# Block-sparse attention feeding a top-1 mixture of experts, one core: pairs of an expert's token slots share one splitting of its weights

## The chip, the core and the metric

The kernel runs on one core of one Trainium2 chip. The metric is device time of one launch in microseconds (us). Its engines are PE (TensorE, matrix products), DVE (VectorE), ACT (ScalarE), POOL (GpSimd) and SP (which issues most transfers); PEld is PE's weight load, which overlaps its products. Each engine works through its own instructions in the order of the program and waits on semaphores for the others.

## The reference: what is computed

Attention over 4 batch elements, 8 heads, 768 positions and 64 columns, in blocks of 32 positions: a query block sees its neighbours, the first and last block and three sampled blocks. The result, 3072 tokens of 512 columns, goes into eight experts, of which each token takes one:

```python
logits = x @ w_gate
e_idx = np.argmax(logits, axis=1)
...
gate_w = probs[np.arange(N), e_idx]
eom = 1.0 / (1.0 + np.exp(-(x @ w_output_gate)))
for e in range(E):
    mask = e_idx == e
    h = np.maximum(x[mask] @ w1[e], 0.0)
    ye = h @ w2[e]
    out[mask] = gate_w[mask, None] * eom[mask, e, None] * ye
```

Worked through with the reference's own inputs, the experts 0 to 7 get 431, 32, 256, 32, 256, 160, 593 and 1312 tokens.

## The kernel before, in words

**Number format.** Products run in 16-bit floats. To keep the precision of 32 bits, each operand is split into a high part and a low part (hi = rounded value, lo = value minus hi), and a product is the sum of three: hi*hi, hi*lo, lo*hi.

**Attention and routing.** 24 tiles of 128 tokens leave the attention in a list of steps. Each tile is written to memory (`xscr`, hi and lo), its expert is chosen (`route_p` to `route_c`), and `route_d` (L757) scatters token number, row and coefficient into `table`, one list for every expert. POOL issues these scatters.

**The plan.** When the last tile is counted, `plan_ops` (L772 to L804) works out on DVE, with one partition for every slot, which expert and which rows of the table a slot of 128 tokens has, and whether the weights in its buffer already belong to that expert. `load_t` (L833 to L840) reads these values into SP's registers.

**The experts.** There are 32 slots, of which 28 (`NSURE`) always run; the other four stand behind a test on the chip (L1168, `used > NSURE`). Slots 0 and 1 are the first of experts 0 and 1 and start before the plan. A slot has 8 pieces of 128 hidden columns. For every piece n:

- `load_w` (L845): SP loads 512 KB of weights, 128 x 1024 32-bit values, unless the buffer already holds this expert (a condition on the transfer). Two buffers, for even and odd slots, hold 8 pieces each.
- `w_h` (L891): ACT writes the high part of the piece, 128 x 1024.
- `w_l` (L898): DVE writes the low part from the piece and the high part. For one piece in eight (`on_pool`), POOL does this instead with two instructions, `w_f` (L887) and the subtraction at L896.
- `p_h` (L909): PE, 12 products 128 x 128 (4 chunks of the 512 columns of the token, three of the four hi/lo products).
- `h_h` (L917) on ACT and `h_l` (L922) on DVE: rectify and split the hidden values of four pieces at a time, 128 x 512.
- `p_y` (L932): PE, 3 products 128 x 512, summed over the 8 pieces of the slot.

Around a slot, `load_x` (L853) is an indirect gather of its 128 token rows, issued by POOL; `x_t` turns them, by a DMA transpose (L860, issued by SP) or for slots 2 and 3 (`PEX`) by PE (L865); `y_o` (L938) on ACT scales the result and `store_y` (L941) on POOL scatters it to the output.

**The order.** `program` writes a step for every piece. In step n stand the split of piece n + 3 (`LEAD`), the first products of piece n, the second products of piece n - 6 (`YL`) and the load of piece n + 18 or so. The gather of a slot stands 14 steps ahead of its first product and its transpose 6 steps. `in_order` makes every engine keep this order.

Of the kernel before, what the change touches and what calls it, by code (L numbers as in the profile page):

```python
# [39 lines left out]
NE = 2  # L40
# [23 lines left out]
# second batch pair: steps of the preparation of V of every half of a block of 128 keys  # L64
# [4 lines left out]
# how the sampled blocks of K come to the pairs of query blocks  # L69
# [4 lines left out]
# first batch pair: step of the preparation of V of every block of 128 keys, whether GpSimd takes part, and whether  # L74
# it comes early in the step
# [19 lines left out]
def tile_kernel(ctx, tc, q, k, v, sampled, wg, wcat, out):  # L95
# [25 lines left out]
    # ---- block lists: which blocks each query block visits, for both gathers  # L121
# [5 lines left out]
    # one partition for every slot  # L127
    PS = NSLOT
    index = const.tile([PS, 3], F32, name="index")
    row0 = const.tile([PS, 1], F32, name="row0")  # L130
    jump = const.tile([PS, 8], F32, name="jump")
    pads = const.tile([PS, 4, 16], F32, name="pads")
    lim = const.tile([1, NE], F32, name="lim")
    base8 = const.tile([128, 8], F16, name="base8")
    tile8 = const.tile([PS, 8], I32, name="tile8")
    vals = const.tile([128, NT, 4], I32, name="vals")
# [5 lines left out]
    # matmuls on ones while the first data is on its way: they raise the clock of the tensor engine  # L142
# [7 lines left out]
    # the table of the exponential is loaded while the first data is on its way  # L150
# [6 lines left out]
    raw = const.tile([128, NB * 3, 2], I32, name="raw")  # L157
# [10 lines left out]
    it = sp.tile([128, 128], I32, name="it")  # L168
    places = sp.tile([1, NSLOT, 3], I32, name="places")
# [8 lines left out]
    def setup_iota():  # L178
# [28 lines left out]
    def setup_dup():  # L207
        # the same block a second or third time
# [13 lines left out]
    def setup_const():  # L222
# [6 lines left out]
        # the list of expert e starts at row e * NTOK  # L229
        nc.vector.tensor_single_scalar(base8, iota128[:, 0:8], NTOK / 128.0, op=ALU.mult)  # L230
        nc.vector.tensor_scalar(lim, iota128[0:1, 0:NE], float(NTOK), 128.0, op0=ALU.mult, op1=ALU.add)
        # tri[k, m] = 1 where k < m
        nc.vector.tensor_scalar(tri, iota128, pcol[:, 0:1], None, op0=ALU.is_gt)

    pw = sp.tile([1, NSLOT, 3], F16, name="pw")

    def setup_vals():
        # rows of the table from one list of slots to the next; the first experts' lists lie a slot further
        nc.gpsimd.memset(jump, float(NTOK))
        nc.gpsimd.memset(jump[:, NE - 1:NE], float(NTOK - 128))  # L240
# [18 lines left out]
        # pairs: 64 (i + 1) - 32 + 32 e; blocks 0 and 23: 736 e  # L259
# [7 lines left out]
    def setup_blocks():  # L267
        nc.vector.tensor_copy(smp, raw[0:1, :, 0])
        sf = sp.tile([128, NB, 3], F32, name="sf")
        nc.vector.tensor_copy(sf.rearrange("p a c -> p (a c)"), raw[:, :, 0])  # L270
        # window position of every query block: qb - s in {-1, 0, 1} or s in {0, 23}
        qbf = sp.tile([128, NB, 3], F32, name="qbf")
        nc.vector.tensor_copy(qbf, qbi)
        dd = sp.tile([128, NB, 3], F32, name="dd")
        nc.vector.tensor_sub(dd, sf, qbf)
        bad = sp.tile([128, NB, 3], F32, name="bad")
        t0 = sp.tile([128, NB, 3], F32, name="t0")
# [4 lines left out]
        # V row of each slot: blk * 32 + r, or the row of zeros at 768  # L282
        # row = s*32 + r + bad*(768 - s*32 - r)
# [5 lines left out]
        # chunk A: [s0 s1 s2 w0], chunk B: [w3 s0 s1 s2]  # L289
# [14 lines left out]
    def setup_rest():  # L304
        # places that no token takes: past the end of the output
# [8 lines left out]
    # state of the routing, one column per tile of 128 tokens  # L314
# [9 lines left out]
    # queries of one batch element, zero in the rows of the other one  # L324
    qz = [[ring.tile([128, 512], F32, name=f"qz{n}_{b}") for b in range(2)] for n in range(RQ)]
# [102 lines left out]
    # ---- attention units; the stages of a unit run in different steps  # L428
# [8 lines left out]
    # o holds sums of P V_hi, of P, and of P V_lo  # L437
# [444 lines left out]
    def on_pool(n):  # L882
        return n in POOLW or n % 8 == 3 and n > 16
# [340 lines left out]
```

## Time and profile before

| what | value |
|---|---|
| time of three runs | 721.76, 726.85, 725.9 us (median 725.9) |
| the profiled execution, span from first to last instruction | 710.4 us |
| its own time beyond the span | not recorded; the three runs have 11.4 to 16.5 us more than this span |
| DVE busy | 630.8 us, 89% |
| PE busy | 586.8 us, 83% |
| ACT, POOL busy | 480.3 us (68%), 428.8 us (60%) |
| DMA | 133.53 MB, mean 188 GB/s |

A row of a group reads: line, engine, operation, tiles out<-in, shapes, xcount, then busy us and mean ns of one, then the idle time of the engine in front and what ended it. A row of the timeline has start, duration, engine, line, operation; where several instructions are merged, xcount. A row of the windows has, for a stretch, the busy time of PE, PEld, DVE, ACT and POOL with their counts, then the granted clock of PE (1.00 is full), the DMA share and GB/s. A row of the waits has the waiting engine and line, what ended the wait, total us, times, longest. Ends of products are modelled: the distance between starts says more than a duration.

### The profile page before, as it was taken

What the parts mean: (1) busy time and instruction counts of PE and PEld (TensorE: products, weight loads), DVE (VectorE), ACT (ScalarE), POOL (GpSimd) and SP (SyncE); (2) the same over time, 40 slices, a digit from 0 to 9 for tenths busy, and PEclk for the clock granted to TensorE, in tenths of its full rate; (3) what the DMA queues carried; (4) which work ended last, traced back from release to release, by engine and by line L of the source; (5) the groups of instructions that cost most, each with busy time, mean ns of one, the idle gap of its engine ahead of it and who ended that gap; (6) DMA issues with size and microseconds to landing.
All of it is one profiled execution on the core that took longest, in us unless ns stands there. A gap on an engine that the chain in (4) does not pass through costs nothing.

```text
span 710.4 us, 22455 instructions
## 1 busy us (share of the span) xinstructions
PE 586.8 (83%) x8214; PEld 383.1 (54%) x8214; DVE 630.8 (89%) x999; ACT 480.3 (68%) x868; POOL 428.8 (60%) x421
## 2 busy tenths in 40 slices
PE   7878797698999888967587888888888887887886
PEld 5444454455655445546365556655555565555554
DVE  5988887788879889979579999999999999999993
ACT  2866776486688787855377676776676676676671
POOL 5556666475468887666666556556466466466461
PEclk7999999999999999987889999999999999999999
DMA  8987999897779999993082694376724724812282
GB/s 223 286 259 237 236 247 304 259 224 187 156 197 276 292 270 308 192 260 53 4 294 52 154 330 157 76 230 198 227 50 137 221 61 147 211 50 60 61 264 70
DMA packets 99054, 133.53 MB, mean 188 GB/s; under 512 B 62075, under 2 KB 69115, under 8 KB 98684
## 3 DMA queue, kind: packets, MB, share of 16 engines
q1 hardware_dynamic: 87196, 94.40, 51.7%
q0 software_dynamic: 11744, 37.64, 16.2%
q8 instruction: 67, 1.10, 0.7%
q14 instruction: 47, 0.39, 0.2%
HBM read 183.87 MB, written 20.49 MB: 288 GB/s over the span
## 4 chain that ended last, share of the span: by engine, by line
DVE 36%; DMA 22%; PE 19%; issue 13%; POOL 4%; ACT 3%; SPq 2%; POOLq 0%; ACTq 0%; DVEq 0%
DVE kr L898 17%; DMA xscr<-xq 9%; DVE ws L898 7%; PE h L909 4%; DVE hl L922 4%; PE S L494 4%; DMA vt<-vscr,vidx 3%; PE y L932 3%; PE T L459 2%; DMA kn<-in_k_dram 2%; DVE pl L473 2%; DMA out_dram<-yo,tab 2%; POOL table L757 2%; DVE mx L500 1%; DMA wide<-in_v_dram 1%
## 5 line engine op out<-in xcount | busy, mean ns | idle before, releaser
L898 DVE SCALAR_TENSOR_TENSOR kr<-r,kr 128x1024 f16<-128x1024 f32 (+1 forms) x144 | 231.4, 1655 | 9.4 <-ACT kr L891 9.3
L891 ACT ACTIVATE kr<-r 128x1024 f16<-128x1024 f32 (+1 forms) x171 | 167.0, 1031 | 11.8 <-DMA r<-in_wcat_dram 9.7
L909 PEld LDWEIGHTS <-kr 128*128 128x128 f16 x2004 | 128.6, 99 | 72.2 <-DVE kr L898 33.3
L909 PE MATMUL h<-qz,kr 128*128 128x128 f16 x1884 | 136.8, 220 | 30.5 <-DVE kr L898 28.4
L941 POOL DMA_INDIRECT out_dram<-yo,tab x28 | 30.0, 1073 | 127.3 <-ACT yo L938 121.4
L898 DVE SCALAR_TENSOR_TENSOR ws<-r,ws 128x1024 f16<-128x1024 f32 (+1 forms) x60 | 102.8, 1761 | 0.0
L932 PE MATMUL y<-kr,hh 128*128 128x512 f16 x334 | 100.3, 382 | 0.0
L506 ACT ACTIVATE P<-S,mx 128x256 f32<-128x256 f32 x176 | 75.1, 486 | 36.4 <-DVE mx L501 33.6
L494 PE MATMUL S<-kr,qz 128*32 128x256 f32 x1408 | 96.6, 393 | 0.0
L896 POOL TENSOR_TENSOR kr<-wf,kr 128x1024 f16<-128x1024 f32 x27 | 72.2, 2674 | 21.8 <-issue 10.7
L473 DVE SCALAR_TENSOR_TENSOR pl<-T,ph 128x512 f16<-128x512 f32 x88 | 60.2, 685 | 17.4 <-ACT ph L466 16.3
L500 DVE TENSOR_REDUCE mx<-S 128x2 f32<-128x512 f32 x88 | 59.5, 676 | 13.5 <-PE S L494 13.4
L932 PE MATMUL y<-kr,hl 128*128 128x512 f16 x167 | 64.0, 383 | 3.1 <-DVE hl L922 3.1
L917 ACT ACTIVATE hh<-h 128x512 f16<-128x512 f32 x56 | 33.2, 592 | 46.1 <-PE h L909 46.1
L909 PEld LDWEIGHTS <-ws 128*128 128x128 f16 x684 | 44.0, 100 | 32.4 <-DVE ws L898 18.6
L891 ACT ACTIVATE ws<-r 128x1024 f16<-128x1024 f32 (+1 forms) x60 | 58.0, 1012 | 2.1 <-PE y L932 2.1
L459 PE MATMUL T<-ident,P 128*128 128x128 f32 x352 | 59.1, 292 | 0.3 <-DVE pl0d L473 0.3
L909 PE MATMUL h<-qz,ws 128*128 128x128 f16 x612 | 45.4, 219 | 16.3 <-DVE ws L898 15.6
L466 ACT ACTIVATE ph<-T 128x512 f16<-128x512 f32 x88 | 54.1, 615 | 5.4 <-PE T L459 5.4
L853 POOL DMA_INDIRECT qz<-xscr,tab x28 | 47.9, 1710 | 11.9 <-DMA tab<-table 7.4
L938 ACT ACTIVATE yo<-y,tab 128x512 f32<-128x512 f32 x28 | 19.2, 687 | 52.9 <-PE y L932 52.9
L494 PEld LDWEIGHTS S<-kr,qz 128*32 128x32 f32 x1408 | 37.3, 110 | 31.2 <-issue 14.8
(233 smaller groups left out, 1178.3 us busy)
## 6 DMA issues: line engine op xcount, KB each, us to landing
r<-in_wcat_dram SPq DMA_DIRECT2D x240, 512.0 KB
qz<-in_q_dram SPq DMA_DIRECT2D x48, 128.0 KB
xscr<-xq SPq DMA_DIRECT2D x48, 128.0 KB
vc<-vscr SPq DMA_DIRECT2D x22, 260.0 KB
vscr<-vn SPq DMA_DIRECT2D x12, 260.0 KB
vscr<-vn SPq DMA_DIRECT2D x6, 520.0 KB
kn<-in_k_dram SPq DMA_DIRECT2D x4, 768.0 KB
vs<-in_v_dram SPq DMA_DIRECT2D x6, 512.0 KB
```

Source lines behind the costliest of these rows:

```text
L459: nc.tensor.transpose(pt[:, 128 * c:128 * c + 128], p[:, 128 * c:128 * c + 128], ident)
L466: nc.scalar.activation(ph[:, 0:w], pt[:, 0:w], AF.Copy, scale=SP_)
L473: nc.vector.scalar_tensor_tensor(pl[:, 0:w], pt[:, 0:w], SP_, self.ph[n][:, 0:w], op0=ALU.mult, op1=ALU.subtract)
L494: nc.tensor.matmul(s[64 * h2 + 32 * qi:64 * h2 + 32 * qi + 32, hp], t[:, 64 * j + 32 * qi:64 * j + 32 * qi + 32], g[:, 1 - qi:3:1 + qi, :, ...
L500: nc.vector.tensor_reduce(mx, self.s, axis=AX.X, op=ALU.max)
L506: nc.scalar.activation(p[:, 256 * hp:256 * hp + 256], self.s[:, hp], AF.Exp, bias=self.mx[:, hp:hp + 1], scale=EXPS)
L853: nc.gpsimd.indirect_dma_start(xgs[s], None, src, bass.IndirectOffsetOnAxis(ap=tabs[s][:, 1:2], axis=0))
L891: nc.scalar.activation(w[:, 0, r], piece(n // 8, n % 8)[:, r], AF.Copy, scale=SW)
L896: nc.gpsimd.tensor_tensor(w[:, 1], ws.pop(("f", n)), w[:, 0], op=ALU.subtract)
L898: nc.vector.scalar_tensor_tensor(w[:, 1, r], piece(n // 8, n % 8)[:, r], SW, w[:, 0, r], op0=ALU.mult, op1=ALU.subtract)
L909: nc.tensor.matmul(hps[n // 4][:, 128 * j:128 * j + 128], w[:, hl, 128 * c:128 * c + 128], x[:, c // 2, xl, c % 2], start=cnt == 0, stop=c ...
L932: nc.tensor.matmul(ys[s], a[:, m], w[:, l, 512:1024], start=n % 8 == 0 and cnt == 0, stop=n % 8 == 7 and cnt == 2)
```

## The change

A *unit* is now a slot or a pair of slots of one expert. Units 0 and 1 stay single slots. 15 units follow that always run: 11 pairs (`NPU`, 256 tokens) and 4 singles (`NSU`), with a single in every fourth place (`PAIR`), so that the order is pair, pair, single, pair, and so on, and the last is a single. Four more pairs (`NIF`) stand behind the test on the chip, which is taken when more than 11 pairs or more than 4 singles are needed. A pair left without two tiles takes a place of the table that no token has.

- `w_h` and `w_l` run once for the 8 pieces of a unit, whether it has one tile or two. `on_pool`, `w_f` and the subtraction on POOL are gone, so DVE writes every low part.
- `p_h`: its 12 products have 256 columns in a pair. `h_h` and `h_l` take two pieces at a time, 128 x 512 in a pair and 128 x 256 in a single. `p_y`: 6 products in a pair, into two banks of the `S` pool.
- `y_o` and `store_y` run for every tile. `load_x` issues a gather for every tile into one buffer (`xbuf[2]`), `x_t` a transpose for every tile.
- `YL` goes from 6 to 4. The gather stands 9 steps ahead (14 before), the transpose 5 (6 before), the load of the table's rows 18 (24 before). Unit 3 is turned by PE in step 19, unit 2 in step 14.
- `plan_ops` has 31 instructions on DVE (15 before) and 19 partitions. The first two units of the plan always load their weights (`places[..., 6] = 100`).
- The scatters of tiles 12 to 15 stand one step apart, not four.

```diff
-NSLOT = 32
-NSURE = 28
+NE = 2
+NPU, NSU, NIF = 11, 4, 4
+NPLAN = NPU + NSU + NIF
+PAIR = [False] * NE + [w % 4 != 2 for w in range(NPU + NSU)] + [True] * NIF
+NSURE = NE + NPU + NSU
...
-YL = 6
+YL = 4
-PLAN = 6, (20,)
+PLAN = 6, (40,)
-POOLW = {8: (2,2,3)}
...
+        nc.gpsimd.memset(places[:, 0:2, 6], 100)
...
+        tabs[u] = rt.tile([128, 2, 4], I32, tag="tab", name=f"tab{u}", bufs=4)
...
+        for m in range(tiles_of(u)):
+            nc.gpsimd.indirect_dma_start(
+                xgs[u][:, m], None, src, bass.IndirectOffsetOnAxis(ap=tabs[u][:, m, 1:2], axis=0))
...
+            t = xbuf[u % 2]
+        for m in range(tiles_of(u)):
+            if u not in PEX:
+                nc.sync.dma_start(t[:, m].rearrange("p (c t) -> p c t", t=128), xg[:, m], transpose=True)
+                continue
...
     def w_l(n, r=slice(0, 1024)):
         w = ws[n]
-        if on_pool(n):
-            nc.gpsimd.tensor_tensor(w[:, 1], ws.pop(("f", n)), w[:, 0], op=ALU.subtract)
-        else:
-            nc.vector.scalar_tensor_tensor(
-                w[:, 1, r], piece(n // 8, n % 8)[:, r], SW, w[:, 0, r], op0=ALU.mult, op1=ALU.subtract)
+        nc.vector.scalar_tensor_tensor(
+            w[:, 1, r], piece(n // 8, n % 8)[:, r], SW, w[:, 0, r], op0=ALU.mult, op1=ALU.subtract)
+    def cols(n):
+        k = 128 * tiles_of(n // 8)
+        return slice(k * (n % 2), k * (n % 2) + k)
...
                 nc.tensor.matmul(
-                    hps[n // 4][:, 128 * j:128 * j + 128], w[:, hl, 128 * c:128 * c + 128],
+                    hps[n // 2][:, cols(n)], w[:, hl, 128 * c:128 * c + 128],
                     x[:, c // 2, xl, c % 2], start=cnt == 0, stop=cnt == 11)
...
+        for m, y in enumerate(ys[u]):
+            k = slice(k0 + 128 * m, k0 + 128 * m + 128)
+            for cnt, (a, l) in enumerate(((hh, 0), (hh, 1), (hl, 0))):
+                nc.tensor.matmul(
+                    y, a[:, k], w[:, l, 512:1024],
+                    start=n % 8 == 0 and cnt == 0, stop=n % 8 == 7 and cnt == 2)
...
-                do(max(t - 24, end), 0, load_t, s, n1 + ahead)
-                do(max(t - 14, end + 1), 1, load_x, s, n1 + ahead)
-            do(XS.get(s, t - 6), 15, x_t, s)
+                do(max(t - 18, end), 0, load_t, u, n1 + ahead)
+                do(max(t - 9, end + 1), 1, load_x, u, n1 + min(ahead, 1))
+            do(XS.get(u, t - 5), 15, x_t, u)
...
-    with tc.If(used > NSURE):
-        emit(program(NSURE, NSLOT), 10 ** 6)
+    with tc.If(more > NPU):
+        emit(program(NSURE, NUNIT), 10 ** 6)
```

How this moves DVE, in the middle of the experts. `r` is the loaded piece, `kr` and `ws` are buffers of split pieces, `h` the hidden values in PE's accumulators, `hh` and `hl` their split. Before, four splits in a row and then the hidden values of four pieces:

```order
L898 SCALAR_TENSOR_TENSOR ws_5929<-r_5353,ws_5929 128x1024
L898 SCALAR_TENSOR_TENSOR ws_5930<-r_5353,ws_5930 128x1024
L898 SCALAR_TENSOR_TENSOR ws_5931<-r_6313,ws_5931 128x1024
L898 SCALAR_TENSOR_TENSOR kr_184<-r_6313,kr_184 128x1024
L922 SCALAR_TENSOR_TENSOR hl_9576<-h_9468,hh_9575 128x512
```

Now, at the place where a single slot (hidden values 128x256) goes over into a pair (128x512):

```order
L984 SCALAR_TENSOR_TENSOR hl_9836<-h_9770,hh_9835 128x256
L954 SCALAR_TENSOR_TENSOR kr_182<-r_7993,kr_182 128x1024
L954 SCALAR_TENSOR_TENSOR kr_183<-r_7993,kr_183 128x1024
L984 SCALAR_TENSOR_TENSOR hl_9883<-h_9819,hh_9882 128x512
L954 SCALAR_TENSOR_TENSOR kr_183<-r_7993,kr_183 128x1024 x2
L984 SCALAR_TENSOR_TENSOR hl_9937<-h_9866,hh_9936 128x512
```

Two splits of a piece now stand between two of the hidden values, where three or four stood; but in a pair each step of PE is for two tiles.

How it moves POOL, also in the middle of the experts. `qz` are the buffers of the gathered and turned tokens, `wf` a piece scaled by POOL. Before, two slots:

```order
L853 DMA qz_0_191<-xscr,tab_8987 128x1024
L887 TENSOR_TENSOR wf_9364<-r_5353,sw_104 128x1024
L941 DMA out_dram<-yo_9405,tab_8638 3072x512
L896 TENSOR_TENSOR kr_183<-wf_9364,kr_183 128x1024
L853 DMA qz_0_187<-xscr,tab_9216 128x1024
L887 TENSOR_TENSOR wf_9583<-r_6313,sw_104 128x1024
L941 DMA out_dram<-yo_9624,tab_8669 3072x512
L896 TENSOR_TENSOR kr_182<-wf_9583,kr_182 128x1024
```

Now, a single and the pairs around it:

```order
L914 DMA qz<-xscr,tab_9737 128x1024 x2
L1013 DMA out_dram<-yo_0_10194,tab_9228 3072x512
L1013 DMA out_dram<-yo_1_10196,tab_9228 3072x512
L914 DMA qz<-xscr,tab_9973 128x1024
L1013 DMA out_dram<-yo_0_10451,tab_9485 3072x512
L1013 DMA out_dram<-yo_1_10453,tab_9485 3072x512
L914 DMA qz<-xscr,tab_10232 128x1024 x2
```

POOL's two instructions on weights are gone, and only gathers and scatters are left, two of each for a pair.

More of the change, by code (lines that the diff above doesn't have):

```diff
@@ L39 @@
 GE = 3
-NE = 2
 SP_ = 256.0
@@ L126, in tile_kernel @@
     ones = const.tile([128, 128], F16, name="ones")
[L128 to L132, printed above, removed]
+    PS = NPLAN
+    index = const.tile([PS, 7], F32, name="index")
+    bins = const.tile([PS, 17], F32, name="bins")
+    start = const.tile([PS, 17], F32, name="start")
     lim = const.tile([1, NE], F32, name="lim")
@@ L323, in tile_kernel @@
     vc = [ring.tile([128, 2, 8, VW], F16, name=f"vc{i}") for i in range(RV)]
-    qz = [[ring.tile([128, 512], F32, name=f"qz{n}_{b}") for b in range(2)] for n in range(RQ)]
+    qzall = ring.tile([128, RQ, 2, 512], F32, name="qz")
+    qz = [[qzall[:, n, b] for b in range(2)] for n in range(RQ)]
     kn, vn = {}, {}
@@ new lines, in plan_ops @@
+        yield nc.vector.tensor_single_scalar(ci[:, 0], ci[:, 0], 1, op=ALU.arith_shift_right)
+        yield nc.vector.tensor_copy(pads[:, 0, 16:32], ci.rearrange("p t e -> p (t e)"))
+        for m, d in enumerate((1, 2, 4, 8)):
+            yield nc.vector.tensor_tensor(
+                pads[:, m + 1, 16:32], pads[:, m, 16:32], pads[:, m, 16 - d:32 - d], op=ALU.add)
+        before = pads[:, 4, 15:32]
+        pairs = pads[:, 4, 23:24]
+        most = sp.tile([PS, 2], F32, name="most")
+        yield nc.vector.tensor_single_scalar(most[:, 0:1], pairs, float(NPU), op=ALU.max)
@@ new lines, in plan_ops @@
+        own = sp.tile([PS, 2, 17], F32, tag="sf", name="own")
+        yield nc.vector.tensor_tensor(own, ge[:, :, 0:17], ge[:, :, 1:18], op=ALU.subtract)
+        tf = sp.tile([PS, 8], F32, name="tf")
+        yield nc.vector.scalar_tensor_tensor(
+            tf, pads[:, 0, 16:24], 2.0, tilef, op0=ALU.mult, op1=ALU.add)
+        yield nc.vector.scalar_tensor_tensor(
+            start[:, 0:8], before[:, 0:8], -2.0, tilef, op0=ALU.mult, op1=ALU.add)
+        yield nc.vector.scalar_tensor_tensor(
+            start[:, 8:16], before[:, 8:16], -2.0, tf, op0=ALU.mult, op1=ALU.add)
@@ new lines, in plan_ops @@
+        ee = sp.tile([PS, 2, 17], F32, tag="qbf", name="ee")
+        yield nc.vector.tensor_tensor(ee, own, bins.unsqueeze(1).to_broadcast([PS, 2, 17]), op=ALU.mult)
+        ec = sp.tile([PS, 2], F32, name="ec")
+        yield nc.vector.tensor_reduce(ec, ee, axis=AX.X, op=ALU.add)
+        yield nc.vector.tensor_tensor(ee[:, 0], own[:, 0], start, op=ALU.mult)
+        row = sp.tile([PS, 2], F32, name="row")
+        yield nc.vector.tensor_reduce(row[:, 0:1], ee[:, 0], axis=AX.X, op=ALU.add)
+        yield nc.vector.scalar_tensor_tensor(
+            row[:, 1:2], at2[:, 0:1], 2.0, row[:, 0:1], op0=ALU.mult, op1=ALU.add)
@@ L797, in plan_ops @@
+        yield nc.vector.tensor_scalar(
+            es[:, 2:3], row[:, 1:2], 128.0, float(EMPTY), op0=ALU.mult, op1=ALU.min)
         yield nc.vector.tensor_copy(es[:, 0:1], ec[:, 0:1])
-        row = sp.tile([PS, 1], F32, name="row")
-        yield nc.vector.tensor_reduce(row, cw, axis=AX.X, op=ALU.add)
         yield nc.vector.scalar_tensor_tensor(
-            es[:, 1:2], ec[:, 1:2], index[:, 2:3], ec[:, 0:1], op0=ALU.max, op1=ALU.not_equal)
-        yield nc.vector.tensor_tensor(es[:, 2:3], row0, row, op=ALU.add)
@@ new lines, in load_t, with load_w @@
+        _, regs[u] = nc.values_load_multi_w_load_instructions(
+            es[w:w + 1, 0:2], engines=[ET.SP], min_val=0, max_val=E - 1)
+        src = table[ds(row[0], 128 * m)].rearrange("(p m) c -> p m c", m=m)
+        after_scatters(nc.sync.dma_start(tabs[u][:, 0:m], src).ins)
+    def load_w(u, j):
+        ev, chg = regs[u]
+        src = wcat[j, ds(ev, 1)].rearrange("o p n -> (o p) n")
+        nc.sync.dma_start(piece(u, j), src, cond=chg)
+    xbuf = [t.rearrange("p b n -> p (b n)").bitcast(F16).rearrange("p (m n) -> p m n", m=2) for t in
+            (qzall[:, n] for n in range(RQ))]
@@ L880, in wring @@
         return wbuf[n % len(wbuf)]
-    def on_pool(n):
-        return n in POOLW or n % 8 == 3 and n > 16
-    def w_f(n):
-        wf = ws["f", n] = ring.tile([128, 1024], F32, tag="vt", name=f"wf{n}", bufs=RV)
-        nc.gpsimd.tensor_tensor(wf, piece(n // 8, n % 8), sw128.to_broadcast([128, 1024]), op=ALU.mult)
     def w_h(n, r=slice(0, 1024)):
```

245 lines of the change are left out of this document (132 added, 113 removed).

## The prediction

> **What bounds the kernel now.** I read the groups of instructions of the experts' stage (from 400 us) first, then busy time by windows, then the waits, and the chain and the timeline for single places.
>
> ```profile
> L898 DVE SCALAR_TENSOR_TENSOR kr<-r,kr 128x1024 f16<-128x1024 f32 x110 | 187.2, 1753 | 0.3 <-ACT kr L891 0.3
> L898 DVE SCALAR_TENSOR_TENSOR ws<-r,ws 128x1024 f16<-128x1024 f32 x45 | 82.7, 1890 | 0.0
> L896 POOL TENSOR_TENSOR kr<-wf,kr 128x1024 f16<-128x1024 f32 x23 | 62.8, 2732 | 16.1 <-issue 9.5 <-DMA r<-in_wcat_dram 6.6
> ```
>
> DVE's split of a piece takes 1.74 us on average here (269.9 / 155). It has almost no idle time in front, so DVE is full. The windows (PE, PEld, DVE, ACT, POOL, then clock, DMA share, GB/s) show one slot, 13.2 us, and a stretch of its own kind:
>
> ```profile
> 385.20:398.40 13.20, 11.04 (x123) 7.61 (x121) 13.20 (x10) 9.31 (x12) 7.45 (x4) 1.00 0.34 62
> 432.00:445.00 13.00, 13.00 (x149) 9.53 (x148) 12.57 (x12) 10.39 (x12) 6.24 (x5) 0.99 0.26 73
> ```
>
> DVE is busy 13.20 of 13.20 us and PE 11.04. Only from 432 to 445, after a stall in which DVE had run ahead, is PE full. There the start of one piece's first products follows the last one's by 1.32 us (440.21 - 438.89):
>
> ```profile
> 438.89 0.83 PE L909 MATMUL h<-qz,kr 128*128 128x128 f16 x12
> 440.21 0.83 PE L909 MATMUL h<-qz,kr 128*128 128x128 f16 x12
> ...
> 700.65 0.59 PE L932 MATMUL y<-ws,hh 128*128 128x512 f16 x2
> 701.29 0.59 PE L932 MATMUL y<-kr,hh 128*128 128x512 f16 x2
> ```
>
> Three second products take 0.64 us (701.29 - 700.65), so the 12 first ones take 0.68. Eight pieces are 10.6 us of PE in a slot of 13.2: some 2.6 us are waiting, 26 times. The waits, from 357 us on, say for whom:
>
> ```profile
> PEld L909 <- DVE kr L898: 33.3, 29, 1.2
> PEld L909 <- DVE ws L898: 18.6, 17, 1.6
> PEld L932 <- DVE hl L922: 16.1, 23, 0.7
> ```
>
> Together 68.0 us, all on DVE. Why DVE is slow stands in the chain and the timeline:
>
> ```profile
> 508.31 3.27 DVE ws L898
> ...
> 508.56 1.91 POOL L887 TENSOR_TENSOR wf<-r,sw 128x1024 f32<-128x1024 f32 x1
> 513.76 1.21 DVE L898 SCALAR_TENSOR_TENSOR kr<-r,kr 128x1024 f16<-128x1024 f32 x1
> ...
> 437.22 3.48 DVE L898 SCALAR_TENSOR_TENSOR kr<-r,kr 128x1024 f16<-128x1024 f32 x3
> 438.74 1.71 POOL L941 DMA_INDIRECT out_dram<-yo,tab  x1 [6.55 <-ACT yo L938]
> ```
>
> A split takes 3.27 us when POOL computes beside it and 1.21 us when it doesn't. A DMA_INDIRECT of POOL does not slow it: three splits around one took 3.48 us, 1.16 each. POOL's help with one piece in eight costs DVE about what it saves.
>
> **The change part by part.** The end is set by PE from the first product of slot 2 to the last second product, and by the scatter behind it:
>
> ```profile
> 360.32 1.03 PE L909 MATMUL h<-qz,kr 128*128 128x128 f16 x12
> ...
> 704.32 0.38 PE L932 MATMUL y<-kr,hl 128*128 128x512 f16 x1
> ...
> span 710.4 us, 22455 instructions
> ```
>
> That is 344.4 us (704.7 - 360.3), and 5.7 us of tail. PE's own work in it is 26 slots x 8 x 1.32 = 274.6, and 6 pieces x 0.64 = 3.9 us of second products left over from slot 1 (the lag YL); the other 65.9 us are waits, which agrees with the 68.0 above.
>
> *PE in the new order.* A pair's piece has 12 products of 256 columns and 6 of 512. No 16-bit product of 256 columns is in the trace; it lies between half of a 512 (0.64 / 3 / 2 = 0.107 us) and two of 128 (2 x 0.68 / 12 = 0.113). I take the upper end: 12 x 0.113 + 6 x 0.213 = 2.64 us, the lower one gives 2.56. So 11 pairs x 8 x 2.64 = 232.3, 4 singles x 8 x 1.32 = 42.2, leftover 4 x 0.64 = 2.6 (YL is 4). PE turns the tokens of unit 3 (16 products, 0.9 us by the distance of the row below to the next product, doubled). Sum 278.0 us. **PE's own work does not shrink; what goes is its waiting.**
>
> ```profile
> 364.46 0.61 PE L865 MATMUL xgp<-ident,qz 128*128 128x128 f16 x8
> 364.91 0.83 PE L909 MATMUL h<-qz,kr 128*128 128x128 f16 x12
> ```
>
> *DVE and ACT.* Other rows of the stage:
>
> ```profile
> L922 DVE SCALAR_TENSOR_TENSOR hl<-h,hh 128x512 f16<-128x512 f32 x44 | 29.9, 679 | 0.2 <-ACT hh L917 0.2
> L891 ACT ACTIVATE kr<-r 128x1024 f16<-128x1024 f32 x132 | 131.2, 1050 | 2.1 <-PE y L932 2.1
> L917 ACT ACTIVATE hh<-h 128x512 f16<-128x512 f32 x44 | 26.0, 592 | 37.7 <-PE h L909 37.7
> L938 ACT ACTIVATE yo<-y,tab 128x512 f32<-128x512 f32 x22 | 15.1, 688 | 42.2 <-PE y L932 42.2
> ```
>
> In a pair, DVE has 1.21 + 0.68 / 2 = 1.55 us a piece and ACT 1.05 + 0.59 / 2 + 2 x 0.69 / 8 = 1.52, both under PE's 2.64. In a single the hidden values are 128 x 256, between half and all of 0.68: DVE 1.38 to 1.55, ACT 1.29 to 1.43, against 1.32. So DVE is over PE by 0.06 to 0.23 a piece in 32 pieces, 2 to 7 us, less what its lead of three pieces hides: I take 2. POOL's 23 subtractions and the scalings ahead of them leave, and with them the slowing of DVE.
>
> *The start.* Unit 2 gathers two tiles, and PE turns both ahead of its first product:
>
> ```profile
> 353.37 0.98 POOL L853 DMA_INDIRECT qz<-xscr,tab  x1 [5.44 <-DMA tab<-table]
> 354.66 1.51 POOL L853 DMA_INDIRECT qz<-xscr,tab  x1 [0.30 <-DMA r<-in_wcat_dram]
> 356.93 1.03 PE L865 MATMUL xgp<-ident,qz 128*128 128x128 f16 x8 [9.75 <-DMA qz<-xscr,tab]
> ```
>
> A second gather goes out 1.3 us after the first, and eight more turns cost 1.0: 2.3 us, and 0.4 for sharing the DMA with weights that unit 2 now always loads: 2.7 us late (bounds 0 and 6). Those weights are issued from 352.9 on and the chain has one landing of 5.3 us, so the second piece is there by 359, split by 361, ahead of the new start at 363.0. The plan's 16 more instructions (2.0 us took 15 of them) lie beside PE's work on units 0 and 1 and the scatters of `route_d`, and cost nothing; if they held the scatters up, 2 us. DVE's extra low part (piece 8) stands in the same place.
>
> ```profile
> 352.92 5.54 SPq L845 DMA_DIRECT2D r<-in_wcat_dram  x10
> 554.67 5.31 DMA r<-in_wcat_dram
> 335.27 0.14 DVE L777 TENSOR_SCALAR ci<-cp 32x8 int32<-32x8 f32 x1
> 337.14 0.13 DVE L804 TENSOR_SCALAR es<-pads 32x1 int32<-32x1 f32 x1
> ```
>
> *Tokens of later units.* A gather and a DMA transpose for every tile, through one gather buffer:
>
> ```profile
> DMA to landing us min/median/max: 4.0/5.0/7.1
> L853 POOL DMA_INDIRECT qz<-xscr,tab x26: 1111/1786/1796, 364.7 to 691.9; - x26
> 420.54 7.33 DMA qz<-qz
> ```
>
> The second gather goes out 1.8 us after the first and lands 5.0 to 7.1 later; its transpose took 7.3 us at the one place where PE waited for it, amid weight loads. That makes 14.1 to 16.2 us. A unit behind a pair has 9 x 2.64 = 23.8 us for it. A pair behind a single (three times) has 2.6 + 8 x 1.32 = 13.2: up to 3.0 us late each, 0 to 9 in all. I take 2.5, since SP and POOL run somewhat ahead of PE. Weights: with these counts nine units load after the plan where seven slots did, 9 x 4.2 MB = 38 MB in 280 us, far below the 389 GB/s of the busy stretch below.
>
> *The sum.* 360.3 + 2.7 + 278.0 + 2 + 2.5 = 645.5 for PE's end, with the tail 651.2 of span, 59 us less than 710.4. The three runs' median lies 15.5 us above the profiled span; I leave that as it is: **725.9 - 59.2 = 666.7 us**. With the lower ends (2.56 a piece, no delays) 652; with the upper ones (start 6, DVE 7, tokens 9) 681.
>
> **The rivals.**
>
> *Tokens come late more often.* The gather buffer is single and each unit's chain starts only when the last unit's transposes have landed. If the three pairs behind singles and the four singles are each 3.0 us late, PE also loses clock behind the wait:
>
> ```profile
> 422.00:423.00 1.00, 1.00 (x13) 0.65 (x11) 1.00 (x2) 0.13 (x1) 0.00 (x0) 1.00 0.99 389
> 430.00:431.00 1.00, 1.00 (x12) 1.00 (x11) 1.00 (x2) 0.96 (x1) 0.98 (x2) 0.50 1.03 414
> ```
>
> Behind the wait of 428 the clock is 0.50 for 3 us, which costs 1.5: 7 x 4.5 - 2.5 = 29 us, 696. For it: that wait. Against it: PE waited for tokens only twice in 24 transposes.
>
> *DVE stays slow.* If the splits keep their 1.74 us (their cause not being POOL), a pair is still PE's (1.74 + 0.34 = 2.08), but a single's piece takes 2.0 instead of 1.32: 32 x 0.7 = 22 us, less a lead, 684. Against it: the 1.21 and 3.27 us above.
>
> *The clock.* A PE that is full for 280 us may be granted less. The lowest 25 us of the stage:
>
> ```profile
> 350.00:375.00 25.00, 17.45 (x183) 12.91 (x183) 16.50 (x14) 17.33 (x22) 14.29 (x9) 0.80 0.64 214
> ```
>
> At 0.80 throughout, 278.0 becomes 347.5, which gives all back: 736. Against it: this stretch has idle PE in it, and the full stretch of 432 to 445 has 0.99. The Trainium skill (TensorE: Matmul & The Clock Gate, Part 1) tells of a limit of 13/16 of the clock when three cores of a die run dense products and says that one or two never trip it; by it this kernel alone keeps 1.00, and a 13/16 would give 731.
>
> *Slower: the part behind the test runs.* Four pairs more, whether needed or not, are 4 x 8 x 2.64 = 84.5 us, and their tokens are gathered only then (16 us): 667 + 100 = 767. It decides from the fifth single or the twelfth pair on. The page shows 28 slots run now, and none behind the test:
>
> ```profile
> L938 ACT ACTIVATE yo<-y,tab 128x512 f32<-128x512 f32 x28 | 19.2, 687 | 52.9 <-PE y L932 52.9
> ```
>
> Against it: by the reference's token counts, without the two first slots, experts 0 to 7 need 3, 0, 2, 1, 2, 2, 5, 11 slots, that is 11 pairs and 4 singles, exactly what is planned. One token at a border of 128 would break it.
>
> **How the numbers follow.** Forecast 0.78, tokens 0.10, DVE 0.04, clock 0.04, the part behind the test 0.04. About 1% is what a measurement can tell. The first three are faster by over 1%: 0.92; the clock's middle (part of the stage only) counts as the same, 0.04; the last is slower, 0.04. The range goes from 652 over the forecast's own 681 to 688, which takes in the DVE case.
>
> **What would show it.** Right: POOL without TENSOR_TENSOR in the experts; the split at 1.1 to 1.3 us; PE busy near 1.0 in each window with clock 1.00; 2.6 us a piece in pairs; the waits of PE on DVE under 10 us; PE's end near 645. Wrong: PE waiting on the transposes (tokens), a split above 1.5 us, a clock below 0.95 in a full window, more than 28 results written.

## The result, and the profile after

| | kernel before | changed kernel | ratio (95% interval) |
|---|---|---|---|
| first measurement, median us | 723.83 (720.88 to 726.85, 4 runs) | 650.73 (644.14 to 656.36, 4 runs) | 0.9009 (0.892 to 0.9099) |
| repeated on another chip | 709.99 (702.24 to 723.25, 11 runs) | 649.85 (645.5 to 656.84, 6 runs) | 0.9208 (0.9145 to 0.927) |

The medians are of all runs; the ratios leave out slow runs, those more than 1.5% above the fastest of their kernel. The change is faster by 8 to 10%. The forecast was 666.7 us, with a range of 652 to 688; 650.73 lies 1.3 us below the range, and 16 us below the forecast. A run lists its span too: in the profiled runs, time is span + 1.8 us (656.36 and 654.6, 645.5 and 643.7; for the kernel before 709.58 and 707.8).

In the stage of the experts the groups of DVE instructions of the changed kernel (line, engine, operation, tiles, shapes, count, then busy us, mean ns, idle in front and its cause), from 369 to 646 us, read:

```profile
L954 DVE SCALAR_TENSOR_TENSOR kr<-r,kr 128x1024 f16<-128x1024 f32 x88 | 104.6, 1223 | 23.0 <-ACT kr L950 22.9
L954 DVE SCALAR_TENSOR_TENSOR ws<-r,ws 128x1024 f16<-128x1024 f32 x30 | 35.9, 1223 | 10.2 <-ACT ws L950 10.2
L984 DVE SCALAR_TENSOR_TENSOR hl<-h,hh 128x512 f16<-128x512 f32 x44 | 30.4, 691 | 54.7 <-ACT hh L978 54.7
L984 DVE SCALAR_TENSOR_TENSOR hl<-h,hh 128x256 f16<-128x256 f32 x17 | 7.2, 422 | 9.2 <-ACT hh L978 9.2
```

A split takes 1.22 us in place of 1.74, there are 118 of them, and DVE has idle time ahead of them. The waits between the first product of unit 2 and the last product have two rows of PE on data:

```profile
PEld L969 <- ACT kr L950: 1.6, 2, 1.4
PE h L969 <- DMA qz<-qz: 0.9, 1, 0.9
```

The 68.0 us of waits on DVE are gone. The windows (PE, PEld, DVE, ACT, POOL, clock, DMA share, GB/s) show the new bound: PE is full at full clock, DVE at 11 to 16 of 20 us. Three of thirteen:

```profile
390.00:410.00 20.00, 20.00 (x145) 13.51 (x144) 11.37 (x13) 10.66 (x14) 4.08 (x4) 1.00 0.36 105
490.00:510.00 20.00, 19.09 (x162) 13.55 (x161) 14.49 (x16) 14.49 (x19) 6.60 (x6) 1.00 0.71 179
590.00:610.00 20.00, 20.00 (x141) 13.64 (x140) 11.37 (x12) 11.03 (x14) 3.50 (x3) 1.00 0.85 243
```

The chain (start, us, what) gives a pair's piece, 1.31 + 1.29 = 2.60 us (`h` are the first products, `y` the second):

```profile
378.14 1.31 PE h L969 x12
379.45 1.29 PE y L999 x6
380.75 1.31 PE h L969 x12
382.06 1.29 PE y L999 x6
```

To compare kernels I cut each profile at three places: the plan's first instruction on DVE (`ci<-cp`), the first product of slot or unit 2, and the end of the last second product. For the changed kernel these are the start of the first two rows and the end of the third (645.21 + 0.38):

```profile
348.70 0.15 DVE L797 TENSOR_SCALAR ci<-cp 19x8 int32<-19x8 f32 x1 [0.18 <-PE cp L794]
...
369.25 0.60 PE L969 MATMUL h<-qz,kr 128*128 128x256 f16 x4
...
645.21 0.38 PE L999 MATMUL y<-kr,hl 128*128 128x512 f16 x1
```

The same places in every profile (us; the runs are told below):

| kernel | plan starts | plan to first product | first to last product | tail | span |
|---|---|---|---|---|---|
| before | 335.27 | 25.05 | 344.4 | 5.7 | 710.4 |
| before, again | 333.40 | 24.25 | 344.4 | 5.7 | 707.8 |
| changed | 348.70 | 20.55 | 276.3 | 9.0 | 654.6 |
| changed, again | 337.31 | 21.92 | 275.8 | 8.7 | 643.7 |
| before, DVE splits all | 348.54 | 22.11 | 292.2 | 5.7 | 668.6 |
| changed, POOL splits one in eight | 348.62 | 21.46 | 284.8 | 9.0 | 663.8 |
| changed + reading work on POOL | 335.48 | 21.10 | 298.6 | 13.0 | 668.2 |
| changed + writing work on POOL | 340.13 | 21.53 | 275.6 | 12.4 | 649.7 |
| changed, free scatters | 333.59 | 21.14 | 275.0 | 8.5 | 638.3 |

From the plan on, the change saves 375.1 - 305.9 = 69 us in the first pair of profiles and 374.4 - 306.4 = 68 in the second. What stands ahead of the plan starts it anywhere between 333 and 349 us in these profiles. The granted clock in the stage of the products is 0.99 to 1.00 in all of them.

### The profile page after: what moved, and what is told of

Read it like the earlier page. It is cut to its first block, busy times and chain, and to the rows that moved or that the text cites. A ratio compares the mean times of both kernels' runs of the same rounds, so it can differ in the third digit from the quotient of the medians.

```text
span 654.6 us, 19342 instructions
## 1 busy us (share of the span) xinstructions
PE 579.6 (89%) x7178; PEld 374.3 (57%) x7178; DVE 466.3 (71%) x968; ACT 401.3 (61%) x794; POOL 280.0 (43%) x375
## 4 chain that ended last, share of the span: by engine, by line
PE 35%; DMA 30%; issue 14%; DVE 9%; ACT 4%; POOL 3%; SPq 2%; POOLq 1%; ACTq 0%; DVEq 0%
PE h L969 13%; PE y L999 11%; DMA xscr<-xq 10%; DMA out_dram<-yo,tab 6%; DMA vt<-vscr,vidx 5%; DMA kn<-in_k_dram 4%; PE S L513 3%; DVE pl L492 2%; PE T L478 2%; DMA qz<-qz 2%; DVE mx L519 1%; DMA qz<-xscr,tab 1%; DMA tab<-table 1%; DMA xT<-xscr 1%; ACT P L525 1%
## 5 line engine op out<-in xcount | busy, mean ns | idle before, releaser
L954 DVE SCALAR_TENSOR_TENSOR kr<-r,kr 128x1024 f16<-128x1024 f32 (+1 forms) x104 | 120.6, 1190 | 25.2 <-ACT kr L950 25.1
L969 PE MATMUL h<-qz,kr 128*128 128x256 f16 (+1 forms) x1080 | 117.9, 259 | 0.0
L950 ACT ACTIVATE kr<-r 128x1024 f16<-128x1024 f32 (+1 forms) x104 | 101.7, 1017 | 4.8 <-DMA r<-in_wcat_dram 4.8
L978 ACT ACTIVATE hh<-h 128x512 f16<-128x512 f32 (+1 forms) x68 | 35.4, 520 | 113.0 <-PE h L969 113.0
L984 DVE SCALAR_TENSOR_TENSOR hl<-h,hh 128x512 f16<-128x512 f32 (+1 forms) x68 | 40.5, 596 | 63.9 <-ACT hh L978 63.9
L999 PEld LDWEIGHTS <-hh 128*128 128x128 f16 x448 | 42.2, 98 | 23.7
L539 PE MATMUL O<-vc,ph 128*64 128x129 f16 x352 | 33.4, 241 | 24.1 <-ACT ob L556 24.0
L954 DVE SCALAR_TENSOR_TENSOR ws<-r,ws 128x1024 f16<-128x1024 f32 (+1 forms) x39 | 43.5, 1140 | 10.2 <-ACT ws L950 10.2
L442 POOL DMA_INDIRECT vt<-vscr,vidx x44 | 43.1, 979 | 11.5 <-issue 8.0
L424 POOL TENSOR_TENSOR kr<-kn,one 128x256 f32<-128x256 f32 x66 | 43.9, 667 | 3.5 <-DMA kn<-in_k_dram 2.9
```

The source lines that it names most:

```text
L424: nc.gpsimd.tensor_tensor(r[:, slot], kn[bp][:, ds(rv, 1)].rearrange("p o n -> p (o n)"), one.to_broadcast([128, 256]), op=ALU.mult)
L539: nc.tensor.matmul(o[64 * h2:64 * h2 + 64, hp, 0:n], w[:, col:col + 64], cv[:, b, 4 * h2 + 2 * hg + hp, 0:n], start=hp == 0 and n == 129, ...
L950: nc.scalar.activation(w[:, 0, r], piece(n // 8, n % 8)[:, r], AF.Copy, scale=SW)
L954: nc.vector.scalar_tensor_tensor(w[:, 1, r], piece(n // 8, n % 8)[:, r], SW, w[:, 0, r], op0=ALU.mult, op1=ALU.subtract)
L969: nc.tensor.matmul(hps[n // 2][:, cols(n)], w[:, hl, 128 * c:128 * c + 128], x[:, c // 2, xl, c % 2], start=cnt == 0, stop=cnt == 11)
L999: nc.tensor.matmul(y, a[:, k], w[:, l, 512:1024], start=n % 8 == 0 and cnt == 0, stop=n % 8 == 7 and cnt == 2)
```

## The experiments

**Both kernels again.** No edit.

> The changed kernel once more, unaltered, for a second profile. If the later start of the plan in its first profile (348.7 us against 335.3) is scatter of single executions, the plan starts within 335 to 345 us here, and the time stays near 651. If the change itself delays the attention, the plan starts at 348 or later again.

> The kernel before once more, unaltered, for a second profile. If the stage of the experts is what the change altered and the attention merely scatters, the time from the first product of slot 2 to the last product is 344 us again (within 3), whatever the plan's start.

The changed kernel started its plan at 337.31 us, 11 us earlier than in its first profile; the kernel before needed 344.4 us of products again. The attention of the run "DVE splits all" below is that of the kernel before (but for the split of piece 8), and its plan starts at 348.54. So the late start in the first profile of the changed kernel is scatter of the attention, not the change. What scatters isn't settled. The pieces of the chain that differ are landings between 130 and 175 us: a gather of V in the changed kernel's first profile, and a store of 15.4 us in another one (of the run "POOL splits one in eight"):

```profile
153.46 13.20 DMA vt<-vscr,vidx
```

```profile
155.79 15.36 DMA xscr<-xq
```

**GpSimd out, nothing shared.** The kernel before, with GpSimd's splits given to DVE:

```diff
-POOLW = {8: (2,2,3)}
+POOLW = {}
...
     def on_pool(n):
-        return n in POOLW or n % 8 == 3 and n > 16
+        return False
```

> The kernel before with one alteration: GpSimd splits nothing, DVE splits all eight pieces of every slot. Theory A (GpSimd's instructions of two operands hold DVE's splits up, and this made DVE the bound): the split falls from 1.74 us to 1.21, DVE needs 8 x 1.21 + 2 x 0.68 = 11.0 us a slot instead of 13.2, 26 slots save 57 us, about 667 us; then the shared splitting is worth the other 16 us. Theory B (the shared splitting is what matters, the split's mean of 1.74 has another cause): DVE needs 8 x 1.74 + 1.36 = 15.3 us a slot, 26 slots cost 54 us more, about 778 us.

663.61 us (658.76 to 670.44), ratio to the kernel before 0.9372 (0.9301 to 0.9442); the changed kernel had 0.9208 beside the same runs of before. DVE got the eighth piece of every slot in addition, and the stage fell from 344.4 to 292.2 us:

```profile
L898 DVE SCALAR_TENSOR_TENSOR kr<-r,kr 128x1024 f16<-128x1024 f32 x155 | 181.8, 1219 | 9.2 <-ACT kr L891 9.1
L898 DVE SCALAR_TENSOR_TENSOR ws<-r,ws 128x1024 f16<-128x1024 f32 x51 | 60.1, 1218 | 6.0 <-ACT ws L891 6.0
L922 DVE SCALAR_TENSOR_TENSOR hl<-h,hh 128x512 f16<-128x512 f32 x53 | 36.3, 684 | 5.0 <-ACT hh L917 5.0
```

The split is at 1.22 us although nothing is shared, as theory A has it. So 52 of the 69 us come from taking GpSimd off the weights, by itself. DVE is close to full with 181.8 + 60.1 + 36.3 = 278.2 of 292.2 us, but PE does not wait for it any more: the waits of PE in this stage have no row on DVE. The longest two are on turned tokens and on ACT's split:

```profile
PE h L909 <- DMA qz<-qz: 8.3, 5, 3.2
PEld L909 <- ACT ws L891: 7.2, 2, 3.6
```

So PE's own work, 278.5 us by the sum of the prediction (274.6 + 3.9), is the bound here already, and the 16 us that sharing adds are mostly such waits.

**Sharing alone.** The changed kernel, GpSimd splitting one piece in eight as before:

```diff
+    def on_pool(n):
+        return n % 8 == 3 and n > 16
+    def w_f(n):
+        wf = ws["f", n] = ring.tile([128, 1024], F32, tag="vt", name=f"wf{n}", bufs=RV)
+        nc.gpsimd.tensor_tensor(wf, piece(n // 8, n % 8), sw128.to_broadcast([128, 1024]), op=ALU.mult)
...
     def w_l(n, r=slice(0, 1024)):
         w = ws[n]
+        if on_pool(n):
+            nc.gpsimd.tensor_tensor(w[:, 1], ws.pop(("f", n)), w[:, 0], op=ALU.subtract)
+            return
```

> The changed kernel with GpSimd splitting one piece in eight again, in pairs and singles, as before: the shared splitting alone. DVE needs for a pair 7 x 1.22 + 2 x 1.9 (held up by GpSimd) + 4 x 0.69 = 15.1 us under PE's 20.9, for a single 7 x 1.22 + 3.8 + 4 x 0.4 = 13.9 against 10.5. Theory (DVE has enough room in a pair): the same as the changed kernel but for 0 to 13 us at the singles, 650 to 663, I take 654; then either half alone gives most of the gain. Rival (GpSimd's two instructions of 1.9 and 2.7 us, in line behind its gathers, bring their piece too late once a unit): 2 to 4 us a unit, 13 units, 676 to 700.

656.94 us (646.76 to 665.63), ratio 0.9156 (0.9079 to 0.9232). The stage takes 284.8 us in the one profile, 9 more than the changed kernel's; the times don't show these 9 us, since the ratio lies no higher than the changed kernel's 0.9208. The splits are slowed, and PE doesn't wait for them; what it waits for is GpSimd's own piece, 9.3 us in all:

```profile
L964 DVE SCALAR_TENSOR_TENSOR kr<-r,kr 128x1024 f16<-128x1024 f32 x73 | 105.9, 1481 | 18.7 <-ACT kr L957 18.7
```

```profile
PEld L979 <- POOL kr L962: 5.2, 4, 2.2
PE h L979 <- POOL kr L962: 4.1, 4, 1.9
```

The size is the theory's, the place the rival's. Sharing alone saves 344.4 - 284.8 = 60 us, GpSimd's leaving alone 52, both 68: each half brings PE close to its own bound, and the second one finds only 9 or 16 us left.

**Reading work on GpSimd.** The changed kernel; for every fourth piece GpSimd runs the two instructions of the kernel before on buffers that nobody else uses:

```diff
+    def g_x(n):
...
+        nc.gpsimd.tensor_tensor(gx[0][:, 1], gx[0][:, 0], sw128.to_broadcast([128, 1024]), op=ALU.mult)
+        nc.gpsimd.tensor_tensor(h[:, 0:1024], gx[0][:, 0], h[:, 1024:2048], op=ALU.subtract)
...
             do(n - LEAD, 7, w_l, n)
+            if n % 4 == 3 and n > 16:
+                do(n - LEAD, 6.5, g_x, n)
```

> The changed kernel, and beside every fourth piece GpSimd does two instructions of two operands that nothing needs (1.9 and 2.7 us, the forms of the kernel before, twice as often as there). The result is not touched. Theory A: the splits that meet them take 3.2 us instead of 1.2, so four of them a unit cost DVE 2.0 us each, 8 us; pairs stay PE's (12.2 + 8 = 20.2 of 20.9 us), the four single units go from 10.5 to 11 + 8 = 19, less a lead of some us: 15 to 34 us slower than the changed kernel, 665 to 685. Rival (the slow splits of before had another cause): splits stay at 1.2 us, and the time at 651 plus at most 5.

**Writing work on GpSimd.** The same, with memsets:

```diff
+        nc.gpsimd.memset(gx[0], 0.0)
+        nc.gpsimd.memset(gx[1], 1.0)
+        nc.gpsimd.memset(gx[0][:, 0], 1.0)
```

> As the run above, but GpSimd's extra work beside every fourth piece is three memsets (2048, 2048 and 1024 columns, about 4.9 us together, as long as the two instructions there), which write and read nothing. Theory A in its narrow form (it is GpSimd's reading of SBUF that holds a DVE instruction with two SBUF inputs up): splits stay at 1.2 us, time within 1% of the changed kernel, 651. Rival (any GpSimd work in SBUF holds DVE up, or GpSimd's queue being occupied delays the gathers): 15 to 34 us slower like the run above.

Reading: 671.21 us (664.51 to 685.34), 21 us over the changed kernel's 649.85 on the same chip. Writing: 649.51 us (639.0 to 664.08), no slower. (Both have some 4 us more of tail, with scatters behind the extra work in GpSimd's queue and behind each other.) The splits of the stage with reading work, then with writing work:

```profile
L954 DVE SCALAR_TENSOR_TENSOR kr<-r,kr 128x1024 f16<-128x1024 f32 x88 | 173.1, 2001 | 4.9 <-ACT kr L950 4.9
```

```profile
L954 DVE SCALAR_TENSOR_TENSOR kr<-r,kr 128x1024 f16<-128x1024 f32 x88 | 104.3, 1221 | 21.9 <-ACT kr L950 21.8
```

One place of each timeline shows how. With reading work, the first two rows of DVE and POOL overlap: two splits take 10.37 us beside four GpSimd instructions that follow each other without a gap (439.04 to 446.9; the fourth row begins at 444.82 and takes 2.12):

```profile
438.81 10.37 DVE L954 SCALAR_TENSOR_TENSOR kr<-r,kr 128x1024 f16<-128x1024 f32 x2
...
439.04 1.90 POOL L965 TENSOR_TENSOR gx<-gx,sw 128x1024 f32<-128x1024 f32 x1
...
444.82 2.12 POOL L966 TENSOR_TENSOR gx<-gx,gx 128x1024 f16<-128x1024 f32 x1
```

With writing work, two splits beside a row of memsets take 2.36 us, 1.18 each:

```profile
439.29 2.36 DVE L954 SCALAR_TENSOR_TENSOR kr<-r,kr 128x1024 f16<-128x1024 f32 x2 [0.25 <-ACT kr L950]
...
440.06 1.81 POOL L964 MEMSET gx<- 128x2048 f32 x1
```

So it is not that GpSimd is busy, nor that it uses SBUF: beside work that reads SBUF the splits are slow, beside work that only writes they are not. The split of the hidden values, which takes one of its two inputs from PE's accumulators (PSUM), is not slowed by the reading work (682 ns on average with it, 691 in the changed kernel). The Trainium skill (SBUF — State Buffer, Who interferes with whom) states this rule, a DVE instruction with two SBUF inputs contends with a GpSimd instruction that reads SBUF and not with one that only writes, and both runs agree with it.

**Splits beside GpSimd's scatters.** Here the other direction: does DVE hold GpSimd up? In the kernel before two scatters into the table took 4.33 and 4.83 us, and splits ran beside them. In the changed kernel, six extra splits behind the plan's first instruction, all into one buffer:

```diff
         yield nc.vector.tensor_single_scalar(ci[:, 0], cp[0:PS, 0:8], 127.0, op=ALU.add)
+        for _ in range(6):
+            nc.vector.scalar_tensor_tensor(
+                dum[:, 0].bitcast(F16)[:, 0:1024], piece(0, 0), SW, piece(0, 1),
+                op0=ALU.mult, op1=ALU.subtract)
```

> The changed kernel with six splits (128 x 1024, two inputs in SBUF, 1.22 us each, results unused) on DVE right behind the plan's first instruction, beside GpSimd's last five scatters into the table. Theory: DVE instructions with two SBUF inputs hold GpSimd's issue of indirect transfers up, as the two scatters of 4.3 and 4.8 us in the kernel before beside back-to-back splits; then at least one scatter takes over 3.5 us here, where the changed kernel has none over 1.9. Rival: the issue of a scatter doesn't depend on DVE (the long ones had another cause): all stay at 1 to 1.9 us. In both cases the experts start 7 us later by DVE's own time.

And six reduces, `nc.vector.tensor_reduce(dum[:, 0, 0:1], piece(0, 0), axis=AX.X, op=ALU.max)`:

> As the run above with six reduces (128 x 1024, one input in SBUF, some 1.2 us each) instead of the splits. Theory (two SBUF inputs are what holds GpSimd up): all scatters at 1 to 1.9 us. Rival (any DVE work on SBUF does): one scatter at least over 3.5 us as with the splits.

657.35 and 651.79 us, and in both no scatter over 1.9 us. The theory as put falls: splits beside scatters are not enough. But the six splits took 7.50 us, one every 1.26 us, where three in the kernel before took 3.47, one every 1.13: writing one buffer, each waited for the one ahead, and left a gap. So both were made again with a place of its own for every result:

```diff
+        for i in range(6):
+            nc.vector.scalar_tensor_tensor(
+                dum[i // 4].rearrange("p a n -> p (a n)").bitcast(F16)[:, 1024 * (i % 4):1024 * (i % 4) + 1024],
+                piece(0, 0), SW, piece(0, 1), op0=ALU.mult, op1=ALU.subtract)
```

> Six splits on DVE behind the plan's first instruction as in the run of the same kind before, but each into a place of its own, so that none waits for the one ahead (there they followed each other every 1.26 us and every scatter slipped in at 0.97; in the kernel before, the splits beside the long scatters followed each other every 1.13 us). Theory (an instruction with two SBUF inputs keeps GpSimd out, and GpSimd gets in only at a gap or beside an instruction that reads PSUM): the splits follow each other every 1.13 us, and a scatter that starts among them ends only after the sixth: one of at least 3.5 us, up to 7.5. Rival (the long scatters had another cause): all at 0.97 to 1.9 us again.

> As the run above with six reduces of one SBUF input, each into a place of its own. Theory (two SBUF inputs): all scatters at 0.97 to 1.9 us though the reduces follow each other without a gap. Rival (any dense DVE work keeps GpSimd out): a scatter of over 3.5 us here too.

Splits without a gap, DVE and POOL:

```profile
339.15 6.88 DVE L800 SCALAR_TENSOR_TENSOR dum<-r 128x1024 f16<-128x1024 f32 x6
...
338.86 1.14 POOL L776 DMA_INDIRECT table<-vals,place  x1 [0.30 <-issue]
340.30 6.59 POOL L776 DMA_INDIRECT table<-vals,place  x1 [0.30 <-issue]
347.20 0.97 POOL L776 DMA_INDIRECT table<-vals,place  x1 [0.30 <-issue]
```

Reduces without a gap:

```profile
336.40 6.85 DVE L800 TENSOR_REDUCE dum<-r 128x1 f32<-128x1024 f32 x6
...
337.07 0.97 POOL L776 DMA_INDIRECT table<-vals,place  x1 [0.30 <-issue]
338.34 0.97 POOL L776 DMA_INDIRECT table<-vals,place  x1 [0.30 <-issue]
```

The scatter that meets the splits ends at 346.89, 0.9 us behind the sixth split's end at 346.03; beside the reduces it takes 0.97. Both theories came out as put, in one profile each: DVE being busy isn't enough, and neither are splits with gaps. But splits without a gap don't hold every scatter up. In the run of the spare pairs, told below, a scatter to the output falls among six of them and ends after 1.55 us, with four splits still to come:

```profile
638.17 6.90 DVE L954 SCALAR_TENSOR_TENSOR kr<-r,kr 128x1024 f16<-128x1024 f32 x6 [4.06 <-ACT kr L950]
...
638.72 1.55 POOL L1013 DMA_INDIRECT out_dram<-yo,tab  x1 [8.74 <-ACT kr L950]
```

In all the profiles only scatters into the table took more than 2.6 us; what sets them apart was not tested. The time itself (656.0 us with the splits and 653.15 with the reduces, two runs each) doesn't tell the two apart, since the extra instructions, which the plan waits for, take 6.9 us in both.

**Free scatters.** The changed kernel, with the scatters to the output declared independent:

```diff
+            tc.declare_no_dep(i, group="out", reason="rows differ")
+            tc.add_to_no_dep_group("out", i)
```

> The changed kernel, its scatters to the output declared independent of each other (the rows differ). Theory: at the end the second scatter of the last pair waits until the first one has landed (2.5 to 3.5 us), so the tail behind the last product falls from 9.0 and 8.7 us in the two profiles to about 6, and the time from 650 to about 647 (less than single executions scatter). Rival: the landing of one scatter takes as long as the wait, and the tail stays at 8 to 9 us.

641.17 us (639.89 to 652.88). The tail is 8.5 us, as the rival has it. The last scatters of the changed kernel (first two rows) wait 6.2 and 2.5 us for landings, and the last goes out 3.2 us behind the last product (648.81 - 645.59); with free scatters (the third row, of the other timeline) it goes out 1.0 us behind it (630.77 - 629.78). But what follows it takes 7.5 us (638.3 - 630.77) in place of 5.8 (654.6 - 648.81):

```profile
645.29 1.00 POOL L1013 DMA_INDIRECT out_dram<-yo,tab  x1 [6.19 <-DMA out_dram<-yo,tab]
648.81 0.98 POOL L1013 DMA_INDIRECT out_dram<-yo,tab  x1 [2.52 <-DMA out_dram<-yo,tab]
```

```profile
630.77 0.98 POOL L1013 DMA_INDIRECT out_dram<-yo,tab  x1 [6.17 <-ACTq L1241]
```

The time is 9 us below the changed kernel's (which ran on other chips), but the profile has none of it where the edit is: products 275.0, tail 8.5, and a plan that starts at 333.59. That the edit speeds the attention up isn't shown; its early plan lies in the scatter above. My expectation was also wrong on one point: the last unit is a single, so the waiting scatters are the second one of the pair ahead of it and the single's own.

**The price of the slower rival.** The changed kernel with the test altered, so that the four spare pairs run empty:

```diff
-    with tc.If(more > NPU):
+    with tc.If(more > NPU - 1):
```

> The changed kernel with the test on the chip altered (more > 10 instead of > 11), so that the four spare pairs run although no token is in them. It gives the price of the forecast's slower rival: 4 x 8 x 2.64 = 84.5 us of products and about 16 us until the first of their tokens are there, 100 us more than the changed kernel, about 750 us. Rival: the loads run ahead of the test or the empty rows are cheaper, under 90 us more.

741.56 us (736.49 to 746.62), 91 more than the changed kernel on other chips; the products take 367.4 us (359.46 to 726.81), 91.5 more. 32 pieces of 2.60 are 83.2; most of the rest is the wait for the first spare tokens, of which the chain shows a gather and a transpose:

```profile
646.39 8.17 DMA qz<-xscr,tab
...
654.57 4.24 DMA qz<-qz
```

## Why the prediction was right in kind and 16 us too high, point by point

| term, us | predicted | first profile | second profile |
|---|---|---|---|
| plan to first product (25.05 + 2.7) | 27.7 | 20.6 | 21.9 |
| first to last product (278.0 + 2 + 2.5) | 282.5 | 276.3 | 275.8 |
| tail | 5.7 | 9.0 | 8.7 |
| sum from the plan on | 315.9 | 305.9 | 306.4 |
| plan's start | 335.3 | 348.7 | 337.3 |
| time beyond the span | 15.5 | 1.8 | 1.8 |
| time | 666.7 | 656.4 | 645.5 |

- **What bounds it: right, and shown.** GpSimd's help held DVE up, and without it the split is at 1.22 us (forecast 1.1 to 1.3). Putting the reading work back slows it again; writing work doesn't.
- **PE's own work: right.** Forecast 2.64 us a piece in pairs, measured 2.60, by which 88 pieces need 3.5 us less. I had taken the upper of two bounds (2.64 and 2.56); the truth lay in the middle.
- **DVE in singles, tokens late: too high.** Of 2 + 2.5 us, the first profile has 0.9 us of waits on tokens, the second 0.3 us on DVE. I read this as DVE's lead of three pieces, and SP and POOL running ahead, covering the singles; no run takes the lead away.
- **The start: the step that failed.** I had it 2.7 us later than the 25.05 us before, from two gathers and eight turns more, and costed the plan's 16 more instructions at nothing or 2 us. It came 2.3 to 4.5 us earlier. Two parts went opposite ways and partly hid each other. Ahead of the last scatter of the table the changed kernel is 8.2 us shorter: that scatter goes out 3.5 us behind the plan's start (352.22), beside the plan's own small instructions, which last from 348.70 to 354.00. In the kernel before the plan was over after 2.0 us, gapless splits began, two scatters were long, and the last one went out at 346.96, 11.7 us behind the plan's start:

```profile
337.20 3.47 DVE L898 SCALAR_TENSOR_TENSOR kr<-r,kr 128x1024 f16<-128x1024 f32 x3
...
337.19 4.33 POOL L757 DMA_INDIRECT table<-vals,place  x1 [0.30 <-issue]
341.82 4.83 POOL L757 DMA_INDIRECT table<-vals,place  x1 [0.30 <-issue]
```

  Behind the last scatter it is longer than I had it: 17.0 us to the first product (369.25 - 352.22) where the kernel before has 13.4 (360.32 - 346.96), so 3.7 more for my 2.7 (5.9 more in the second profiles). I had taken the scatters' time for fixed, and did not ask why two of them took over four times as long as the others. That gapless splits held these two up agrees with the experiment above; that the long plan is what spares the new kernel this is read from the rows and not tested. It isn't the whole account either: "DVE splits all", with the short plan and scatters of 3.80 and 4.84 us, needs 22.1 us from the plan on, about as long as the changed kernel; its last scatter goes out 6.6 us behind the plan's start (355.14 - 348.54), with one scatter fewer left by then than in the kernel before.
- **The tail: not in the sum.** 3 us more. The rows show a pair's second scatter waiting for its first, and the last single for both; but with the scatters free of each other the tail was 8.5 us, so what makes it longer stays open. I carried the old tail over without asking what stands behind the last product in the new order.
- **The base: wrong.** I carried 15.5 us "beyond the span" from before to after as if it belonged to the kernel. By the profiled runs that list both, time is 1.8 us more than span, so the other 13.7 us lay between the profiled execution and the three timed ones, not inside a run. What made the timed ones slow isn't known: in that first measurement the kernel before took 720.9 to 726.9 us, on three other chips its medians are 710 to 715, and the changed kernel shows no such difference (650.7 and 649.9). This is the largest single error. With the 9.5 us of the terms, less 2.0 for a later plan, it makes the 21.2 us between 666.7 and 645.5. Without it the sum would have said 653.
- **The rivals.** Tokens late more often: 0.9 us in all. A clock below 1: the windows have 1.00 for 280 us of full PE. DVE slow: 1.22 us. Slower: the spare pairs didn't run; their price is 91 us, not 100.
- **What I had not asked:** which half of the change brings the gain. Either alone brings most of it, 52 and 60 of 68 us. The prediction has POOL's help costing DVE "about what it saves"; taking it away made the stage 52 us shorter, so it cost far more than it saved.

## What to carry to other kernels

Work given to a second engine has to be priced on the first one too: in the kernel before the stage was 52 us longer with an eighth of the splits on GpSimd than with all of them on DVE. When two edits both lift the same bound, price each alone; the second one is worth only what is left up to the next bound, here PE's 276 us. A profiled execution and a median of other runs are two samples: a difference between them belongs to the kernel only if a run's own span and time show it.

## What the runs showed of the hardware

- A DVE split (two SBUF inputs) waits while GpSimd's instructions of two operands follow each other without a gap: two splits took 10.37 us beside four of them, and 2.36 us beside memsets.
- Splits without a gap can hold a scatter's issue up over several instructions: 6.59 us beside six splits into a place each. With splits 1.26 us apart (1.22 us each) every scatter took 0.97 to 1.14 us. This was seen for scatters into the table alone; a scatter to the output took 1.55 us among six gapless splits. The scatters did not slow the splits: in the kernel before, three around a scatter to the output took 3.48 us, and three beside a scatter that was held up 3.47.
- An instruction of DVE that reads PSUM for one input lets such a scatter in: in the kernel before the scatters of 4.33 and 4.83 us end 0.2 us behind the end of the split of hidden values (`hl<-h,hh`, 0.67 us) that follows the splits (341.52 against 341.28, and 346.65 against 346.41):

```profile
340.61 0.67 DVE L922 SCALAR_TENSOR_TENSOR hl<-h,hh 128x512 f16<-128x512 f32 x1
...
345.74 0.67 DVE L922 SCALAR_TENSOR_TENSOR hl<-h,hh 128x512 f16<-128x512 f32 x1
```

- The Trainium skill (SBUF — State Buffer, Who interferes with whom) infers that tensor_tensor, an operation of two inputs, does not stall the writing of descriptors for GpSimd's transfers, because it takes only the read side of the shared ports. No run here tests that: tensor_tensor stands beside scatters only in short instructions (128x256 at most). With scalar_tensor_tensor, the splits' operation, which has two inputs as well, the issue of a scatter into the table took 6.59 us against 0.97 beside reduces, so for that operation and these scatters the measurement says otherwise.
